# Attention with packed keys and a channel mix: first sequence by halves of its heads, weights' signs on ScalarE

## The chip, the cores and the metric

The kernel runs on one core of a Trainium2 chip. The time is device microseconds from launch to end; three runs of the kernel before gave 596.43, 597.06 and 598.03 (median 597.06). Beside these runs one execution was recorded by the profiler; its span, from the first to the last instruction, is 594.0 us. Engines: TensorE (PE, with its weight load PEld), VectorE (DVE), ScalarE (ACT), GpSimd (POOL), SyncE (SP, which issues DMAs).

## The reference

Shapes: batch 8, 8 heads, 576 rows, head size 64, 32 packed rows; model width 512, inner width 1024. All in fp32.

```python
def sm_attn(qq, kk, vv):
    s = scale * np.matmul(qq, kk.transpose(0, 1, 3, 2))
    s = s - np.max(s, axis=-1, keepdims=True)
    a = np.exp(s)
    a = a / (np.sum(a, axis=-1, keepdims=True) + 1e-09)
    return np.matmul(a, vv)
p_packed = sm_attn(p, k, v)
out = sm_attn(q, p_packed, p_packed)
# heads side by side: x is (8, 576, 512); x_prev is x one row later, zero first
xk = mu_k * x + (1.0 - mu_k) * x_prev
xr = mu_r * x + (1.0 - mu_r) * x_prev
k = np.maximum(xk @ w_k, 0.0)
v = k * k @ w_v
r = 1.0 / (1.0 + np.exp(-(xr @ w_r)))
return r * v
```

The three weights arrive as float64 (two 32-bit words each).

## The kernel before

The 8 x 576 rows are cut into nine blocks of 512 rows for the channel mix, so a block spans two sequences except for the first, which lies in the first sequence alone. Of a block TensorE makes `gates` (4 tiles of 128 rows against w_r, 4 parts of the width each), `keys` (8 tiles of the inner width) and `values` (8 x 4 tiles). Each of these 80 groups is three fp32r products of 128x512, because every operand is kept as a high and a low part (`_h`, `_l`): 240 products a block, in lines 936 to 938, 976 to 978 and 1005 to 1007.

A sequence's attention stands between them. k and q come in pairs of heads, are turned so that the head size lies on the partitions (for sequences 1 and 2 by TensorE, `transposed_on_pe` and `first_transposed`; for the others by VectorE in blocks of 32, `transposed`), `front` makes the first scores against p (line 503), `weights_of` the softmax, line 532 the packed rows, `scores` (for the first sequence `half_scores`, which takes half of the rows at a time) the second scores, `back` their softmax. Line 746 puts the result into x, and `mix` makes xk and xr from it. In the first sequence mu is multiplied into the packed rows (`shared`), and `mixed_on_pe` (line 806) lets TensorE make xk and xr directly from the attention weights `a2t`; `rest_of_first` makes the last 65 columns of x.

`convert` turns a piece of a weight (128 x 512 float64, loaded as `st`) into fp32: ScalarE scales the upper word (line 309), VectorE shifts it (311), puts the sign in (313), adds the top bits of the lower word (315); ScalarE writes the high part (319) and VectorE the low one (321). There are 20 pieces: 4 of w_r, 8 of w_k, 8 of w_v.

Nothing of the order is left to a scheduler on the chip: `Flow` runs the whole program as a list of parts, each with a rank, keeps an estimated clock for each engine, and writes the instruction that it thinks can start first. The numbers RANK_..., FIRST, HOLD_V and HOLD_S set ranks and patience. While TensorE has no work in the head, `fill` writes small products of the identity matrix (`spare`, line 1085), until the fourth tile of the first block's gates. Small pools of buffers (raw 3, kq 4, vt 2, staged 4, PSUM pa 2 and m 4) decide when loads and products may start. SP issues every DMA, by line 227.

## Time and profile before

| | us |
|---|---|
| median of three runs | 597.06 |
| span of the profiled execution | 594.0 |
| TensorE busy | 584.2 (98%) |
| VectorE busy | 370.9 (62%) |
| ScalarE busy | 309.2 (52%) |
| first gate product / last product of all | 37.67 / 589.93 |

A busy share is an average over stages with different limits, and products overlap in TensorE, so that one takes longer (about 0.39 us) than the distance to the next. For TensorE the distance from start to start is therefore what counts. An fp32 product (a fill, a score) stands in the trace as two passes: 78 fills in the program are 156 in the trace.

### The profile page before, as it was taken

The numbers are of one execution on the slowest core, as the hardware profiler recorded it, in microseconds if no ns is written. First come the engines' busy times: TensorE is split into PE (matmuls) and PEld (weight loads), VectorE is DVE, ScalarE is ACT, GpSimd is POOL, SyncE is SP. The second block draws the span as 40 slices with busy tenths as digits, with TensorE's granted clock in tenths as the row PEclk, the third lists the DMA queues.
The fourth block names the chain that finished last, engine by engine and source line by source line (L and its number), as shares of the span: only waits on it lengthen the run. The fifth ranks groups of instructions, "written<-read, shape, count | busy, mean of one in ns | idle before, by whom it ended". The sixth has DMA issues, their size and how long they took to land.

```text
span 594.0 us, 10276 instructions
## 1 busy us (share of the span) xinstructions
PE 584.2 (98%) x3965; PEld 458.9 (77%) x3965; DVE 370.9 (62%) x721; ACT 309.2 (52%) x548; POOL 2.1 (0%) x22
## 2 busy tenths in 40 slices
PE   9999999999999999999999999999999999999997
PEld 8776767787778777777777787777788888888885
DVE  2698999956692788867874698269314712641321
ACT  3557884644663458468537392548425613721410
POOL 0000000000000000000000000000000000000000
PEclk9999999999999999999999999999999999999999
DMA  8988460764727076486076375200100010001001
GB/s 214 266 207 258 164 139 17 162 173 73 150 46 189 12 154 143 129 143 141 3 195 135 65 140 134 58 1 1 72 1 1 1 72 0 1 0 72 0 1 71
DMA packets 164095, 56.51 MB, mean 95 GB/s; under 512 B 141000, under 2 KB 155344, under 8 KB 164048
## 3 DMA queue, kind: packets, MB, share of 16 engines
q1 hardware_dynamic: 164048, 55.87, 39.3%
q8 instruction: 31, 0.51, 0.4%
q14 instruction: 16, 0.13, 0.1%
HBM read 42.86 MB, written 12.98 MB: 94 GB/s over the span
## 4 chain that ended last, share of the span: by engine, by line
PE 80%; DVE 13%; SPq 3%; DMA 1%; issue 1%; ACT 1%; DVEq 0%
PE ph L936 10%; PE pvo L1005 10%; PE ph L937 10%; PE ph L938 10%; PE pvo L1007 10%; PE pvo L1006 10%; PE pr L976 5%; PE pr L977 5%; PE pr L978 5%; SPq L227 3%; DVE m L313 2%; DVE m L315 2%; PE pa L532 2%; PE pa L746 2%; PE pa L687 1%
## 5 line engine op out<-in xcount | busy, mean ns | idle before, releaser
L936 PE MATMUL ph<-xk,wk_h 128*128 128x512 f32 x288 | 114.8, 399 | 0.0
L1005 PE MATMUL pvo<-wv_h,sq 128*128 128x512 f32 x288 | 113.8, 395 | 0.0
L937 PE MATMUL ph<-xk,wk_h 128*128 128x512 f32 x288 | 112.5, 391 | 0.0
L938 PE MATMUL ph<-xk,wk_l 128*128 128x512 f32 x288 | 112.3, 390 | 0.0
L1006 PE MATMUL pvo<-wv_l,sq 128*128 128x512 f32 x288 | 112.2, 389 | 0.0
L1007 PE MATMUL pvo<-wv_h,sq 128*128 128x512 f32 x288 | 112.1, 389 | 0.0
L954 DVE CAST sq<-r 128x512 fp32r<-128x512 f32 x72 | 30.0, 416 | 122.0 <-ACT r L950 119.4
L947 ACT ACTIVATE r<-ph 128x512 f32<-128x512 f32 x72 | 43.0, 597 | 85.8 <-PE ph L938 85.5
L1005 PEld LDWEIGHTS pvo<-wv_h,sq 128*128 128x128 f32 x288 | 54.0, 188 | 16.5 <-issue 5.4
L936 PEld LDWEIGHTS ph<-xk,wk_h 128*128 128x128 f32 x288 | 54.1, 188 | 16.0 <-issue 4.1
L1007 PEld LDWEIGHTS pvo<-wv_h,sq 128*128 128x128 f32 x288 | 54.1, 188 | 11.4
L938 PEld LDWEIGHTS ph<-xk,wk_l 128*128 128x128 f32 x288 | 54.1, 188 | 11.4
L937 PEld LDWEIGHTS ph<-xk,wk_h 128*128 128x128 f32 x288 | 54.1, 188 | 11.0 <-DVE xk L843 0.6
L1006 PEld LDWEIGHTS pvo<-wv_l,sq 128*128 128x128 f32 x288 | 54.1, 188 | 10.7
L976 PE MATMUL pr<-wr_h,xr 128*128 128x512 f32 x144 | 57.5, 399 | 0.4 <-DVE sig L1016 0.3
L901 DVE SCALAR_TENSOR_TENSOR x<-xt,mus,x 128x64 f32<-128x64 f32 (+7 forms) x120 | 54.0, 495 | 6.0 <-ACT x L897 5.9
L977 PE MATMUL pr<-wr_l,xr 128*128 128x512 f32 x144 | 56.2, 390 | 0.0
L978 PE MATMUL pr<-wr_h,xr 128*128 128x512 f32 x144 | 56.1, 390 | 0.0
L897 ACT ACTIVATE x<-xt,mus 128x64 f32<-128x64 f32 (+7 forms) x120 | 54.4, 514 | 0.1
L987 ACT ACTIVATE sig<-pr 128x512 f32<-128x512 f32 x36 | 21.4, 601 | 60.7 <-PE pr L978 47.4
L956 DVE TENSOR_TENSOR sq<-r,sq 128x512 fp32r<-128x512 f32 x72 | 49.4, 686 | 1.4
L1016 DVE TENSOR_TENSOR sig<-pvo,sig 128x512 f32<-128x512 f32 x36 | 24.0, 687 | 39.0 <-PE pvo L1007 39.0
(102 smaller groups left out, 693.6 us busy)
## 6 DMA issues: line engine op xcount, KB each, us to landing
out<-sig SPq DMA_DIRECT2D x36, 256.0 KB, 2.6
raw<-in_k SPq DMA_DIRECT2D x96, 72.0 KB, 2.7
raw<-in_q SPq DMA_DIRECT2D x96, 72.0 KB, 2.8
st<-in_moe_w_k SPq DMA_DIRECT2D x8, 512.0 KB, 5.2
st<-in_moe_w_v SPq DMA_DIRECT2D x8, 512.0 KB, 4.7
vt<-in_v SPq DMA_DIRECT2D x24, 160.0 KB, 3.4
away<-blocks SPq DMA_DIRECT2D x12, 288.0 KB, 2.7
vt<-in_v SPq DMA_DIRECT2D x24, 128.0 KB, 3.8
```

The lines of the kernel that those rows point to most:

```text
L897: nc.scalar.mul(x32[:, o:o + n], xts[b, c][:, 1 + s:1 + s + n], mus[:, j, c:c + 1])
L901: nc.vector.scalar_tensor_tensor(x32[:, o:o + n], xts[b, c][:, s:s + n], mus[:, j + 1, c:c + 1], x32[:, o:o + n], op0=ALU.mult, op1=ALU.add,)
L936: nc.tensor.matmul(ph, wk_h[:, c, fs], xh, start=(c == 0), stop=False)
L937: nc.tensor.matmul(ph, wk_h[:, c, fs], xl, start=False, stop=False)
L938: nc.tensor.matmul(ph, wk_l[:, c, fs], xh, start=False, stop=(c == NC - 1))
L956: nc.vector.tensor_tensor(hl[:, 1, :], r, hl[:, 0, :].bitcast(F32), op=ALU.subtract)
L976: nc.tensor.matmul(pr, xh[:, ts_], wr_h[:, c, :], start=(c == 0), stop=False)
L977: nc.tensor.matmul(pr, xh[:, ts_], wr_l[:, c, :], start=False, stop=False)
L978: nc.tensor.matmul(pr, xl[:, ts_], wr_h[:, c, :], start=False, stop=(c == NC - 1))
L1005: nc.tensor.matmul(pv[t], sh, wv_h[:, f, :], start=(f == 0), stop=False)
L1006: nc.tensor.matmul(pv[t], sh, wv_l[:, f, :], start=False, stop=False)
L1007: nc.tensor.matmul(pv[t], sl, wv_h[:, f, :], start=False, stop=(f == NF - 1))
```

## The change

- The first sequence is worked by halves of its heads (`first_side(h)`, two pairs of heads each) and not by halves of its rows. Its loads come in the order k, q of pairs 0 and 1, k of pairs 2 and 3, v, q, v. p is loaded with zeros between its heads, so that two heads' 32 packed rows are one product of 64 columns; the packed rows are masked to a block diagonal.
- Its second scores lie token-major: 112 or 128 rows of q on the partitions and 64 columns for a pair's two heads (`CHUNKS`, 5 x 128 = 640 columns in all). The softmax runs along the free dimension without VectorE's transposes; TensorE turns the result back.
- mu is loaded broadcast over partitions by POOL's queue (`first_constants`), multiplied with the packed rows by VectorE, and `mixed_on_pe` makes two of the four parts of xr or xk with four products of 64 rows and 512 columns. The loads of p (first sequence) and of mu's rows are issued by ScalarE.
- `first_gates` does the first two parts of the width for three tiles, then the other two, then the fourth tile.
- In `convert` ScalarE scales the lower word in place (line 329 after), which leaves the top bits as an integer, and uses Prelu with a slope so that the sign comes with the scaling (331); VectorE joins both in one step (334). The limit 29.829 lets all 20 pieces go this way.
- EARLY = 1: k and q of the second sequence are loaded with 32 columns a time and turned by VectorE, as those of the later sequences; its attention works in blocks from there on.
- All ranks have new numbers, and some are added.

```diff
+    RANK_LATE7 = 3.494
...
+    def load(dst, src, issue, us, queue="queue"):
+        yield queue, issue, None, None
+        dict(queue=nc.sync, scalar=nc.scalar, gpsimd=nc.gpsimd)[queue].dma_start(dst, src)
...
-    EARLY = 2
+    EARLY = 1
...
+        pieces_split.append(event)
+        by_act = len(pieces_split) < RANK_LATE13
+        if by_act:
+            yield act(n)
+            nc.scalar.activation(w0, w0, AF.Copy, scale=2.0 ** -29 * (1 - 2.0 ** -22), bias=-0.5)
         yield act(n)
-        nc.scalar.activation(m.bitcast(F32), w1.bitcast(F32), AF.Copy, scale=2.0 ** -112)
-        yield vec2(n)
-        nc.vector.tensor_scalar(m, m, 3, None, op0=ALU.logical_shift_left)
-        yield vec(n, after=0.0)
-        nc.vector.scalar_tensor_tensor(m, w1, 0x80000000, m, op0=ALU.bitwise_and, op1=ALU.bitwise_or)
-        yield vec(n, after=0.0)
-        nc.vector.scalar_tensor_tensor(m, w0, 29, m, op0=ALU.logical_shift_right, op1=ALU.bitwise_or)
+        nc.scalar.activation(m.bitcast(F32), w1.bitcast(F32), AF.Prelu, scale=2.0 ** -112, alpha=2.0 ** 32)
+        if by_act:
+            yield vec(n)
+            nc.vector.scalar_tensor_tensor(m, m, 3, w0, op0=ALU.logical_shift_left, op1=ALU.bitwise_or)
+        else:
+            yield vec2(n)
+            nc.vector.tensor_scalar(m, m, 3, None, op0=ALU.logical_shift_left)
+            yield vec(n, after=0.0)
+            nc.vector.scalar_tensor_tensor(m, w0, 29, m, op0=ALU.logical_shift_right, op1=ALU.bitwise_or)
...
+    def first_loads():
+        flow.spawn(first_packed(), 5)
+        for h in range(2):
+            for j in (2 * h, 2 * h + 1):
+                flow.spawn(first_pair(k, "kT", j, "xk"), FIRST_K[h])
+                flow.spawn(first_pair(q, "qT", j, "xk" if j == NPR - 1 else "raw"), FIRST_Q[h])
+            flow.spawn(values_of(0, h), FIRST_V[h])
...
+    def first_side(h):
...
+        for hf in range(2):
+            for j, half in enumerate(HALVES):
+                nc.tensor.matmul(
+                    s1[half, hf, :HS], pts[0][1][:, j0 + j, :], ts["kT", 0, j0 + j][1][:, hf * HS:(hf + 1) * HS],
+                    start=True, stop=True,
+                )
...
+        yield from weights_of(0, h, slot, s1, sm)
...
+                nc.tensor.matmul(
+                    pv[rows], aT[:n, c, rows], vt[:n, pr, c * D:(c + 1) * D], start=(c == 0), stop=(c == 4),
+                )
...
+        nc.vector.scalar_tensor_tensor(
+            pm, pv.unsqueeze(1).broadcast_to([P, 2, D]), rs[:, h:h + 1], firsts["mask"], op0=ALU.mult, op1=ALU.mult,
+        )
...
+        nc.tensor.transpose(pT, pm, ident)
+        ppT = firsts["ppT"][:, h]
+        yield act(P)
+        nc.scalar.copy(ppT, pT)
...
+        s2 = banks(slot).rearrange("p a b -> p (a b)")
+        for k, (at, _) in enumerate(CHUNKS):
+            for j in range(2):
+                nc.tensor.matmul(
+                    s2[:, k * P + 64 * j:k * P + 64 * j + 64], ts["qT", 0, j0 + j][1][:, at:at + P],
+                    ppT[:, 64 * j:64 * j + 64], start=True, stop=True,
+                )
...
+        nc.vector.tensor_reduce(m2, s2, axis=AX.X, op=ALU.max)
+        yield vec(n)
+        nc.vector.tensor_tensor(e, s2, over, op=ALU.subtract)
+        flow.give("pa", slot)
+        yield act(n, table="exp")
+        nc.scalar.activation(e, e, AF.Exp, scale=scale)
+        yield vec(n)
+        nc.vector.tensor_reduce(m2, e, axis=AX.X, op=ALU.add)
...
+        nc.vector.tensor_tensor(e, e, over, op=ALU.mult)
...
+        for k, (at, rows) in enumerate(CHUNKS):
+            bank, col = (0, at) if k < 4 else (1, 0)
+            nc.tensor.transpose(back_[:, bank, col:col + rows], e[:rows, k], ident[:rows, :rows])
+        flow.give("xk", se)
+        a2 = firsts["a2"][1][:, h]
+        last = CHUNKS[4][0]
+        yield act(last)
+        nc.scalar.copy(a2[:, 1:1 + last], back_[:, 0, :last])
+        yield act(S - last, after=0.0)
+        nc.scalar.copy(a2[:, 1 + last:], back_[:, 1, :S - last])
...
+        for j, res, tag in ((2, xrs, "xr"), (0, xks, "xk")):
+            flow.spawn(mixed_on_pe(h, j, res, tag), RANK_MIX if tag == "xr" else RANK_KEYS)
...
+        for h in range(2):
+            firsts["mu", h] = (yield from flow.take("sig"))
+        for h in range(2):
+            t = tile_([P, 4, P], F32, "sig", firsts["mu", h], "mub")
+            for j, mu in ((2, mu_r), (0, mu_k)):
+                for c in range(2):
+                    at = (2 * h + c) * P
+                    yield from load(
+                        t[64 * c:64 * c + 64, j], mu[at:at + P].unsqueeze(0).broadcast_to([64, P]), 1.0, 0.02, "gpsimd"
+                    )
...
+        nc.vector.tensor_scalar(t[:, 1::2], t[:, 0::2], -1.0, 1.0, op0=ALU.mult, op1=ALU.add)
...
+        nc.vector.tensor_tensor(t, t, pm.unsqueeze(1).broadcast_to([P, 4, P]), op=ALU.mult)
...
-    def mixed_on_pe(hf, j, res, tag, first):
...
+    def mixed_on_pe(h, j, res, tag):
...
+        slot = yield from flow.take("pa")
+        yield pe(2.0)
+        px = banks(slot)
+        for t in range(2):
+            for c, half in enumerate(HALVES):
+                nc.tensor.matmul(
+                    px[:, c, :TB], shares_of[half, j + t, :], a2[half, h, 1 - t:1 - t + TB], start=(t == 0), stop=(t == 1),
+                )
...
+            yield act(TB, after=multiplied)
+            nc.scalar.copy(xh, x)
+            yield vec(TB)
+            nc.vector.tensor_tensor(xl, x, xh.bitcast(F32), op=ALU.subtract)
...
+        opened = []
+        for part, (cs, tiles) in enumerate(((range(2), range(3)), (range(2, 4), range(3)), (range(4), range(3, 4)))):
+            for t in tiles:
+                if part != 1:
+                    slot = yield from flow.take("m")
+                    opened.append((slot, ps.tile([P, DM], F32, name="pr", tag=f"m{slot}")))
+                slot, pr = opened[t]
+                ts_ = slice(t * P, (t + 1) * P)
+                for c in cs:
+                    yield from flow.wait(("xr", 0, c), ("wr", c, 0))
+                    if part == 1 and flow.keep_busy:
+                        flow.keep_busy = 0.0
+                        flow.give("m", 3)
+                    yield pe(0.683)
+                    flow.now.t -= flow.LAG
+                    _, xh, xl = xrs[0, c]
+                    nc.tensor.matmul(pr, xh[:, ts_], wr_h[:, c, :], start=(c == 0), stop=False)
+                    nc.tensor.matmul(pr, xh[:, ts_], wr_l[:, c, :], start=False, stop=False)
+                    nc.tensor.matmul(pr, xl[:, ts_], wr_h[:, c, :], start=False, stop=(c == NC - 1))
```

On TensorE, from the first scores of the second kind (`qT`, `ppT`) to the first gate products, before:

```order
L667 MATMUL pa<-qT,ppT 32x288 x8
L455 MATMUL pq<-ident,raw 128x96 x6
L1085 MATMUL spare<-ident 128x128 x5
L667 MATMUL pa<-qT,ppT 32x288 x8
L1085 MATMUL spare<-ident 128x128 x20
L415 MATMUL pa<-ident,raw 128x96 x6
L1085 MATMUL spare<-ident 128x128 x2
L415 MATMUL pa<-ident,raw 128x96 x6
L1085 MATMUL spare<-ident 128x128 x5
L806 MATMUL pa<-a2t,pms 64x288 x16
L1085 MATMUL spare<-ident 128x128 x7
L976 MATMUL pr<-wr_h,xr 128x512
```

Now, at the same place (`both` holds the packed rows, `e` the attention weights, `mub` mu times the packed rows; line 610 the scores, 643 the turning back, 956 the mixing products, 1112 the gates), from the second half's scores on:

```order
L610 MATMUL pa<-both,qT 128x64 x10
L643 MATMUL pa<-ident,e 128x112 x4
L643 MATMUL pa<-ident,e 128x128
L1248 MATMUL spare<-ident 128x128 x4
L956 MATMUL pa<-a2t,mub 128x512 x4
L1248 MATMUL spare<-ident 128x128 x9
L1112 MATMUL pr<-wr_h,xr 128x512
```

The second sequence's transposes (`ident,raw`) are gone from this place, and the first half's turning back stands behind the second half's scores.

On ScalarE, from the exp of the first sequence's second softmax (`e`) to the first gate input (`xr`), before (418 copies turned k, 309 and 319 are conversions):

```order
L713 ACTIVATE e<-e 128x576
L418 COPY kT<-pa 128x576
L319 CAST wr_h<-m 128x512
L418 COPY kT<-pa 128x576
L841 CAST xr<-pa 128x288 x4
```

Now:

```order
L628 ACTIVATE e<-e 128x640
L329 ACTIVATE st<-st 128x512
L331 ACTIVATE m<-st 128x512
L329 ACTIVATE st<-st 128x512
L600 COPY both<-pT 128x128
L331 ACTIVATE m<-st 128x512
L329 ACTIVATE st<-st 128x512
L343 CAST wr_h<-m 128x512
L331 ACTIVATE m<-st 128x512
L343 CAST wr_h<-m 128x512
L648 COPY a2t<-pa 128x448
L650 COPY a2t<-pa 128x128
```

Eight conversion steps of w_r now stand between the exp and the copies of the first half's attention weights; three more and the second half's exp follow before the first `xr`.

On VectorE, around the last product of that softmax, before (722 the last product, 725 the transpose behind it) and then now (636 the last product; 334 and 345 are conversions):

```order
L720 RECIPROCAL m_441<-m_441 128x18
L711 TENSOR_TENSOR e<-e,m_473 128x576
L722 TENSOR_TENSOR e<-e,m_441 128x576
L315 SCALAR_TENSOR_TENSOR m<-st,m 128x512
L725 STREAM_TRANSPOSE a2t<-e 128x2x288
```

```order
L634 RECIPROCAL m_364<-m_364 128x20
L334 SCALAR_TENSOR_TENSOR m<-m,st 128x512
L636 TENSOR_TENSOR e<-e,m_364 128x640
L695 TENSOR_TENSOR mub<-mub,pm 128x512
L334 SCALAR_TENSOR_TENSOR m<-m,st 128x512
L345 TENSOR_TENSOR wr_l<-m,wr_h 128x512
```

A conversion step stands ahead of the product, and no transpose behind it.

## Rows read from the trace of the kernel before

**Rows 1.** The page's first part: busy us, share of the span, instructions.

```profile
PE 584.2 (98%) x3965; PEld 458.9 (77%) x3965; DVE 370.9 (62%) x721; ACT 309.2 (52%) x548; POOL 2.1 (0%) x22
```

**Rows 2.** Timeline of TensorE, end: start, us, line, out<-in, shapes, count [idle before].

```profile
587.66 0.39 PE L1006 MATMUL pvo<-wv_l,sq 128*128 128x512 f32 x1
...
589.93 0.39 PE L1007 MATMUL pvo<-wv_h,sq 128*128 128x512 f32 x1
```

**Rows 3.** Timeline of TensorE, the head.

```profile
11.46 1.20 PE L503 MATMUL pa<-kT,pt 64*32 64x288 f32 x32
...
17.89 0.90 PE L532 MATMUL pa<-vt,aT 128*32 128x64 f32 x40
...
20.43 0.33 PE L553 MATMUL pa<-ident,pm 128*128 128x128 f32 x1
...
23.88 0.71 PE L667 MATMUL pa<-qT,ppT 64*32 64x288 f32 x16
...
27.40 4.73 PE L1085 MATMUL spare<-ident 128*128 128x128 f32 x40
...
34.67 1.48 PE L806 MATMUL pa<-a2t,pms 32*64 32x288 f32 x32
...
37.67 0.47 PE L976 MATMUL pr<-wr_h,xr 128*128 128x512 f32 x1
```

**Rows 4.** Windows: stretch, us, busy PE, PEld, DVE, ACT, POOL, PEclk, DMA share, GB/s.

```profile
7.00:20.00 13.00, 12.28 (x199) 10.60 (x198) 3.74 (x10) 6.06 (x13) 0.00 (x0) 1.00 0.84 206
...
20.00:116.00 96.00, 92.43 (x796) 68.46 (x793) 91.41 (x184) 65.96 (x130) 0.30 (x3) 1.00 0.64 173
```

**Rows 5.** Timelines of VectorE and TensorE where the second block's gates start.

```profile
114.69 0.69 DVE L919 TENSOR_TENSOR xr<-x,xr 128x512 fp32r<-128x512 f32 x1
...
116.31 0.47 PE L976 MATMUL pr<-wr_h,xr 128*128 128x512 f32 x1
```

**Rows 6.** SP's timeline, then loads of q and k to 26 us: ns min/median/max, landing.

```profile
1.18 4.94 SPq L227 DMA_DIRECT2D raw<-in_k  x8
...
L227 SPq DMA_DIRECT2D raw<-in_q x8: 430/569/1852, 10.7 to 17.6; - x8
...
DMA to landing us min/median/max: 2.8/3.6/6.7
```

**Rows 7.** Lines by form of VectorE: busy us, mean ns of one | idle before.

```profile
L400 DVE STREAM_TRANSPOSE kT<-raw 128x576 f32<-128x576 f32 x24 | 17.7, 752 | 0.0
L315 DVE SCALAR_TENSOR_TENSOR m<-st,m 128x512 uint32<-128x512 uint32 x20 | 13.8, 688 | 0.4
...
L722 DVE TENSOR_TENSOR e<-e,m 128x576 f32<-128x576 f32 x16 | 11.8, 744 | 0.0
...
L311 DVE TENSOR_SCALAR m<-m 128x512 uint32<-128x512 uint32 x20 | 8.3, 415 | 5.3 <-ACT m L309 5.3
```

**Rows 8.** Lines by form of ScalarE.

```profile
L768 ACT COPY xt<-pa 128x576 f32<-128x576 f32 x28 | 30.9, 1167 | 23.5 <-PE pa L746 23.3
...
L309 ACT ACTIVATE m<-st 128x512 f32<-128x512 f32 x20 | 13.4, 686 | 6.1 <-DMA st<-in_moe_w_r 2.7 <-DMA st<-in_moe_w_v 1.8 <-DMA st<-in_moe_w_k 1.4
...
L713 ACT ACTIVATE e<-e 128x576 f32<-128x576 f32 x16 | 10.8, 680 | 7.2 <-DVE e L711 7.2
```

**Rows 9.** Timeline of TensorE after the gates' start: where other work stands between products.

```profile
40.59 0.48 PE L976 MATMUL pr<-wr_h,xr 128*128 128x512 f32 x1
...
42.14 1.37 PE L806 MATMUL pa<-a2t,pms 32*64 32x224 f32 x32
...
46.59 0.72 PE L806 MATMUL pa<-a2t,pms 32*64 32x288 f32 x8
...
48.82 0.50 PE L976 MATMUL pr<-wr_h,xr 128*128 128x512 f32 x1
...
72.38 1.45 PE L415 MATMUL pa<-ident,raw 96*128 96x96 f32 x12
...
85.67 1.21 PE L687 MATMUL pa<-qT,ppT 64*32 64x288 f32 x32 [0.16 <-ACT ppT L556]
```

More of the change, by code (lines that the diff above doesn't have):

```diff
@@ L416, in transposed_on_pe @@
         flow.give(raw_space, raw_slot)
-        yield act(S)
-        nc.scalar.copy(t.rearrange("p (a b) -> p a b", a=2), pT[:, :, :HS])
+        if b == 0 and pr < RANK_LATE14:
+            done = flow.t
+            yield vec(HS)
+            nc.vector.tensor_copy(t[:, :HS], pT[:, 0, :HS])
+            one = flow.t
+            yield act(HS, after=done)
+            nc.scalar.copy(t[:, HS:], pT[:, 1, :HS])
+            flow.now.t = max(flow.t, one)
+        else:
+            yield act(S)
+            nc.scalar.copy(t.rearrange("p (a b) -> p a b", a=2), pT[:, :, :HS])
         flow.give("pa", slot)
@@ L484, in packed, with first_packed @@
         flow.set(("pt", b))
+    def first_packed():
+        sp = yield from flow.take("tmp")
+        pin = tile_([P, NPR, 2, NP], F32, "tmp", sp, "pin")
+        nc.gpsimd.memset(pin, 0.0)
+        for o in range(0, P, 32):
+            hh, dh = divmod(o // 32, 2)
+            yield from load(
+                pin[o:o + 32, :, hh, :],
+                p[0, hh::2, :, 32 * dh:32 * dh + 32].rearrange("pr n d -> n pr d"),
+                0.5, 0.1, "scalar",
+            )
+            if o < 96:
+                back_to_issue("scalar")
+        slot = yield from flow.take("tmp")
+        pt = tile_([P, NPR, 2 * NP], F32, "tmp", slot, "pt")
+        yield vec(2 * P)
+        nc.vector.transpose(pt.rearrange("p a b -> p (a b)"), pin.rearrange("p a r b -> p (a r b)"))
+        flow.give("tmp", sp)
+        pts[0] = slot, pt
+        flow.set(("pt", 0))
@@ L801, in first_products @@
-    def first_products(px, n, a2, terms):
-        for term, (at, weights) in enumerate(terms):
-            for pr in range(NPR):
-                own = slice(32 * pr, 32 * pr + 32)
-                for h, half in enumerate(HALVES):
-                    nc.tensor.matmul(
-                        px[pr // 2][half, pr % 2, :n], weights(own, h), a2[own, h, at:at + n],
-                        start=(term == 0), stop=(term == len(terms) - 1),
-                    )
-    def mixed_on_pe(hf, j, res, tag, first):
-        a2 = first["a2"][1]
-        yield from flow.wait("pms")
+    def mixed_on_pe(h, j, res, tag):
+        a2 = firsts["a2"][1]
+        yield from flow.wait(("pms", h))
@@ L815, in mixed_on_pe @@
         if tag == "xk":
             yield from flow.wait(("mixed", 1, "xr"))
[L818 to L819 removed]
+        shares_of = firsts["shares", h]
         space = "xk" if tag == "xk" else "sq"
[L821 to L826 removed]
@@ new lines, in mixed_on_pe @@
+        flow.set(("mixed", h, tag))
+        multiplied = flow.t
+        for c in range(2):
+            sx = yield from flow.take(space)
+            hl = tile_([P, 2, TB], F32R, space, sx, tag)
+            xh, xl = hl[:, 0, :], hl[:, 1, :]
+            x = px[:, c, :TB]
+            yield act(TB, after=multiplied)
+            nc.scalar.copy(xh, x)
+            yield vec(TB)
+            nc.vector.tensor_tensor(xl, x, xh.bitcast(F32), op=ALU.subtract)
+            if c:
+                flow.give("pa", slot)
+            res[0, 2 * h + c] = sx, xh, xl
+            flow.set((tag, 0, 2 * h + c))
@@ new lines, in rest_of_first @@
+    def rest_of_first():
+        n = S - TB
+        yield from flow.wait(*(("mixed", h, tag) for h in range(2) for tag in ("xr", "xk")))
+        sx, a2 = firsts["a2"]
+        slot = yield from flow.take("pa")
+        yield pe(0.7)
+        px = banks(slot)
+        for h in range(2):
+            for c, half in enumerate(HALVES):
+                nc.tensor.matmul(
+                    px[:, c, h * P:h * P + n + 1], firsts["pm", h][1][half], a2[half, h, TB:], start=True, stop=True,
+                )
+        for h in range(2):
+            flow.give("pm", firsts["pm", h][0])
+            flow.give("sig", firsts["mu", h])
+        flow.give("sig", firsts["both"])
@@ L1039, in all_loads @@
     def all_loads():
-        for b in range(B):
+        first_loads()
+        for b in range(1, B):
             flow.now.rank = lrank(b)
@@ L1078, in attn_pack_channel_mix @@
     weights()
[L1079 removed]
+    flow.spawn(first_constants(), 10.01)
+    flow.spawn(shares(), RANK_LATE12)
     flow.spawn(channel_mix(), 50)
```

305 lines of the change are left out of this document (153 added, 152 removed).

## The prediction

> **What bounds the kernel now.** I read the page first: TensorE is busy for 98% of the span [rows 1]. Busy is no verdict, so next came the pitch of the product stream. In its steady part ten 128x512 products start in 2.27 us (587.66 to 589.93), 0.227 us each [rows 2]. The channel mix needs 9 blocks x 240 = 2160 of them, 490.3 us. The first gate product starts at 37.67 [rows 3], the last product of all at 589.93 [rows 2]: 552.3 us, so about 62 us of TensorE after 37.67 go to other things (attention of the later sequences, the first sequence's mix, waits). The tail behind 589.93 is 4.1 us. So the span is start of the gates + 490.3 + the other work + tail, and the change can move only the first and the third.
>
> The head is a chain of latencies: fills keep TensorE busy while it waits (40 passes of them at 27.40) [rows 3]. The windows show which engine it waits for: from 20 to 116 us VectorE is busy 91.4 of 96 us, ScalarE 66.0 [rows 4]. At the end of that stretch is a second meeting point: the last part of the second block's gate input leaves VectorE at 114.69 + 0.69, and the second block's gates start at 116.31 [rows 5], so this part is ready some 3 us before the fourth product group needs it. A gain in the head would be lost there again if VectorE kept its work.
>
> **The change, part by part.**
>
> *The head (term A).* Before, the first score products wait for eight k loads, issued over 4.94 us [rows 6], and start at 11.46; the products with v start at 17.89, the second scores at 23.88, the mixing products at 34.67, the gates at 37.67 [rows 3]. Afterwards one half of the heads goes ahead alone. Four k loads fewer bring its start 2.5 us forward, to 9.0. From 11.46 to 17.89 stand 6.4 us for both halves; one half saves one max (0.74) [rows 7]: 5.7. The products with v take 0.9 [rows 3], the scaling behind them 0.4 (17.89 + two such sets and what lies between, to 20.43), the other half's products, which now stand ahead on TensorE, 1.2 (the price of 32 passes of 288 columns) [rows 9], the transpose 0.33 and its copy 0.3 [rows 3]: 17.8. Transposes of the other heads' q in front cost 0.5: 18.3. The token-major scores (10 products, 20 passes, each with its own 128 columns of weights and 64 moving columns) are in no row. A fill pass of 128 moving columns takes 0.118 us [rows 3], so 20 passes take 2.4 at most, and half of that, by columns, at least; the weights are the fill's, so I take the middle, 1.8: 20.1. The softmax over 640 columns goes by the rows of 576: max 0.83, subtraction 0.83, exp 0.76, sum 0.83, small steps 0.4, a conversion step ahead of the last product 0.69, product 0.83: 5.2, 25.3 [rows 7, 8]. Five transposes, 0.7: 26.0. Two copies on ScalarE stand behind up to three conversion steps (1.7) and take 0.8: 28.5. The four mixing products of 64 rows and 512 columns: 8 passes of 4 x 0.118 [rows 3], two side by side, 1.9: 30.4. Cast 0.6, subtraction 0.69: 31.7. Hand-offs not in the blocks above, some twelve at 0.05, 0.6: the gates start at 32.3. A = 37.67 - 32.3 = 5.4. The weights don't set this: k, q and v of the first sequence are 3.5 MB and the first piece of w_r 0.5; at 206 GB/s [rows 4] they are in by about 21, and the other three pieces come at 2.5 us each.
>
> *TensorE after the start of the gates (term B).* What goes: the transposes of the second sequence, 2.24 between the first two groups of three gate products (37.67 to 40.59, less 0.68), 1.3 at 72.38, and two lots of six later at half of that; 4.8. The rest of the first sequence's mix: 1.37 at 42.14, 2.23 from 46.59 to 48.82 with its wait for VectorE, and a like set later which I price the same; 5.8 [rows 3, 9]. What comes: five transposes 0.7, three sets of mixing products 5.7 and, from the order of instructions, two waits, 0.5 before the second gate input and 0.6 before the last mixing set; 7.5. B = 10.6 - 7.5 = 3.1. The attention of sequences two to eight costs TensorE the same as before.
>
> *Conversions.* A piece loses two VectorE steps, 0.42 and 0.69 [rows 7], and gains a ScalarE step. VectorE: -22.1 for 20 pieces, +6.0 for eight transposes of the second sequence [rows 7], +1.5 for four copies of k at half a row of 576: 91.4 becomes about 77, in a stretch that is to shrink from 96 to 87 us. So the meeting point at 116 can move with TensorE, and no part of A and B is handed back there. ScalarE: the added step works in place on every second word, which no row shows. Below it lies the neighbouring scaling step, 0.69; above it the copies in blocks, 1.17 for 576 columns [rows 8]. I take 0.69, the like operation: +13.7, less 5.4 for eight copies and about 1 elsewhere: 66.0 becomes some 74 of 87. That cover is gone at 13 us more. Prelu in place of Copy has the same two ends, and I price it as Copy.
>
> *Second sequence in blocks.* Its 32 loads read 128-byte runs in place of 16 with 256-byte ones. The DMA engines are at 64% from 20 to 116 us [rows 4], so I cost the bytes at nothing; 16 more issues at the old spacing of 0.62 us [rows 6] are 10 us of SP, which would show as w_k arriving late, against a bound of nothing below.
>
> *Loads on other queues.* p and the rows of mu are issued by ScalarE, mu's copies by POOL; no row has either. On SP a load takes 0.43 to 1.85 us to issue and 2.8 to 6.7 to land [rows 6]. Four p loads from about 2.2 are out at 4.0 at the lower end and in by 7.6, before 9.0. POOL's first four are in between 6 and 16; VectorE has them ahead of its first max (10), so the upper end costs 6 us, the lower none, and I take none.
>
> Sum: 5.4 + 3.1 = 8.5 us. Against the profiled execution's own span, 594.0, that is 585.5; the median of the runs, 597.06, lies 3.0 above that span (what lies around it), hence 588.5.
>
> **The rivals.**
>
> (1) *ScalarE fills the head.* If the in-place step costs 1.17, four of them stand ahead of the first gate input (1.9) and nine more before the gates end, on an engine that has no idle time there: about 5 us back, 593.5. For it: ScalarE has the conversions and the copies of the first sequence in one queue. Against: the like step takes 0.69.
>
> (2) *ScalarE becomes the bound, and the kernel slower.* If both scalings of a piece are dear, 40 steps decide, up to the second block's gates. 74 of 87 us leave 13, 0.33 a step; the gain is another 0.21. Above 0.69 + 0.54 = 1.23 us a step the kernel is slower; at 1.3 it is 3 us, 600. Against: that is above the dearest such row (1.17). For: nothing but that neither step has been run.
>
> (3) *POOL's loads are late.* VectorE's sixth instruction waits for the first four; landing at 16 shifts the whole head by 6: 594.5. For: no DMA of POOL is in the trace. The Trainium skill has a rule that would do this ("SBUF — State Buffer", "SBUF: two separate sides"): while VectorE runs an operation in a two-port mode, POOL cannot write the descriptors of its own DMAs. No run here shows it; by the order of instructions VectorE has only copies out of PSUM and one transpose at that time, so the chance stays small.
>
> (4) *The 64-row products don't run two at a time.* Each mixing set then costs 3.8 and not 1.9: 7.6 more, 596. Against: 32 passes of 288 columns on 64x32 tiles take 1.21 [rows 9], 0.038 each where one alone needs more than a fill's 0.118; so tiles of 64 rows do run side by side.
>
> (5) *No change.* The second meeting point does not move (a late chain of the second sequence, whose loads and transposes now compete for SP and VectorE): 596 to 598.
>
> **How the numbers follow.** Forecast 0.70, own range 583 to 592.5 (scores 0.6 either way, hand-offs and waits 2, a partly slower ScalarE step 2). Rival 1 0.12, rival 2 0.06, rival 3 0.04, rival 4 0.04, rival 5 0.04. A measurement of this kernel tells 0.3%, 1.8 us, from no change. Faster by more than that (below 595.3): 0.70 + 0.12 + 0.04 and half of rival 4, 0.88; same 0.06; slower 0.06. The range that should hold eight in ten reaches up over rivals 1 and 3 and down to the forecast's own end: 583 to 594.5.
>
> **What would show it.** In the profile afterwards the first gate product starts near 32; between it and the first key product lie no waits above about 1 us; VectorE's busy time from 20 us to the second block's gates falls to about 77; the added ScalarE step has a mean below 0.75; VectorE's wait for POOL's loads is under 1 us; the second block's gates start near 107. The prediction is wrong if the gates start after 35, if either scaling takes over 1 us, or if key products wait for w_k, xk or a free bank.

## The result, and the profile after

The changed kernel takes 586.52 us, median of 4 runs (585.96 to 587.72), against 597.37 us of the kernel before beside it (596.43 to 598.03). The ratio is 0.9824, with a 95% interval from 0.9809 to 0.9839: faster by 1.8%. Forecast were 588.5 us and a range from 583 to 594.5. The profiled span goes from 594.0 to 584.0 us.

The page's first part of the changed kernel, busy us and share of the span, answers to [rows 1]:

```profile
PE 576.0 (99%) x3746; PEld 452.8 (78%) x3746; DVE 358.9 (61%) x687; ACT 315.9 (54%) x554; POOL 7.3 (1%) x36
```

VectorE loses 12 us over the whole span, ScalarE gains 7, TensorE has 219 instructions fewer. None of these numbers is the gain; the times on TensorE are. Its timeline in the head, for [rows 3]:

```profile
8.60 1.19 PE L555 MATMUL pa<-kT,pt 128*64 128x288 f32 x8
...
14.23 0.90 PE L576 MATMUL pv<-vt,aT 128*32 128x64 f32 x40 [0.38 <-DMA vt<-in_v]
15.06 1.19 PE L555 MATMUL pa<-kT,pt 128*64 128x288 f32 x8
16.18 0.33 PE L597 MATMUL pT<-ident,pm 128*128 128x128 f32 x1
...
17.30 2.37 PE L610 MATMUL pa<-both,qT 128*128 128x64 f32 x20
...
24.51 2.44 PE L610 MATMUL pa<-both,qT 128*128 128x64 f32 x20
26.80 0.67 PE L643 MATMUL pa<-ident,e 112*128 112x112 f32 x5
...
28.28 1.99 PE L956 MATMUL pa<-a2t,mub 64*128 64x512 f32 x8
30.20 2.27 PE L1248 MATMUL spare<-ident 128*128 128x128 f32 x18
32.23 0.47 PE L1112 MATMUL pr<-wr_h,xr 128*128 128x512 f32 x1
```

The second scores of the first half start at 17.30, those of the other half at 24.51; the first gate product stands at 32.23, where [rows 3] have 37.67. Behind it, TensorE's other work between the gate products (for [rows 9]) and the start of the second block's gates (for [rows 5]):

```profile
37.50 3.71 PE L956 MATMUL pa<-a2t,mub 64*128 64x512 f32 x16
...
42.60 1.99 PE L956 MATMUL pa<-a2t,mub 64*128 64x512 f32 x8 [0.49 <-DVE xr L969]
...
45.41 0.66 PE L985 MATMUL pa<-a2t,pm 64*128 64x65 f32 x8
...
105.79 0.39 PE L1134 MATMUL pr<-wr_h,xr 128*128 128x512 f32 x1
...
579.89 0.39 PE L1165 MATMUL pvo<-wv_h,sq 128*128 128x512 f32 x1
```

From first gates to second gates are 73.56 us, before 78.64. The 10.0 us of the span are 5.44 in front of the first gate product, 5.08 between there and the second block's gates, and 0.5 given back behind them. The tail behind the last product is 4.1 us as before.

The windows (stretch, us, busy PE, PEld, DVE, ACT, POOL, PEclk, DMA share, GB/s) answer to [rows 4]:

```profile
20.00:37.70 17.70, 17.70 (x161) 14.86 (x160) 17.47 (x34) 15.54 (x31) 0.00 (x0) 1.00 1.00 258
20.00:107.00 87.00, 85.96 (x638) 63.98 (x636) 78.27 (x147) 75.63 (x140) 0.31 (x3) 1.00 0.80 194
```

Up to the second block's gates VectorE is busy 78.27 us of 87, ScalarE 75.63: forecast were 77 and 74. The two scalings of a piece, by form on ScalarE over that stretch, stand at the price of [rows 8]'s scaling:

```profile
L329 ACT ACTIVATE st<-st 128x512 uint32<-128x512 uint32 x20 | 13.2, 679 | 0.0
L331 ACT ACTIVATE m<-st 128x512 f32<-128x512 f32 x20 | 13.2, 672 | 0.0
```

TensorE's waits between 32 and 110 us (total, times, longest) are down to three:

```profile
PE pa L956 <- DVE xr L969: 0.5, 1, 0.5
PE pa L802 <- ACT a L788: 0.3, 1, 0.3
PE pvo L1163 <- ACT r L1079: 0.2, 1, 0.2
```

### The profile page after: what moved, and what is told of

It reads as the page before. It is cut to its first block, busy times and chain, and to the rows that moved or that the text cites. A ratio compares the mean times of both kernels' runs of the same rounds, so it can differ in the third digit from the quotient of the medians.

```text
span 584.0 us, 9831 instructions
## 1 busy us (share of the span) xinstructions
PE 576.0 (99%) x3746; PEld 452.8 (78%) x3746; DVE 358.9 (61%) x687; ACT 315.9 (54%) x554; POOL 7.3 (1%) x36
## 4 chain that ended last, share of the span: by engine, by line
PE 81%; DVE 8%; ACT 5%; DMA 2%; issue 2%; SPq 1%; DVEq 0%; ACTq 0%
PE ph L1068 10%; PE pvo L1163 10%; PE ph L1069 10%; PE ph L1070 10%; PE pvo L1164 10%; PE pvo L1165 10%; PE pr L1134 5%; PE pr L1135 5%; PE pr L1136 5%; DVE x L1033 2%; PE pa L911 2%; PE pa L739 1%; SPq L242 1%; PE pa L715 1%; PE pa L864 1%
## 5 line engine op out<-in xcount | busy, mean ns | idle before, releaser
L1163 PE MATMUL pvo<-wv_h,sq 128*128 128x512 f32 x288 | 114.0, 396 | 0.2 <-ACT r L1079 0.2
L1163 PEld LDWEIGHTS pvo<-wv_h,sq 128*128 128x128 f32 x288 | 54.1, 188 | 17.8 <-issue 6.3
L1070 PEld LDWEIGHTS ph<-xk,wk_l 128*128 128x128 f32 x288 | 54.1, 188 | 11.4
L1165 PEld LDWEIGHTS pvo<-wv_h,sq 128*128 128x128 f32 x288 | 54.1, 188 | 11.4
L1134 PE MATMUL pr<-wr_h,xr 128*128 128x512 f32 x128 | 50.5, 395 | 0.0
L1135 PE MATMUL pr<-wr_l,xr 128*128 128x512 f32 x128 | 49.9, 390 | 0.0
L1136 PE MATMUL pr<-wr_h,xr 128*128 128x512 f32 x128 | 49.8, 389 | 0.0
L1082 ACT ACTIVATE r<-r 128x512 f32<-128x512 f32 x72 | 45.4, 631 | 2.1
```

The costliest lines, as they stand in the source:

```text
L1070: nc.tensor.matmul(ph, wk_l[:, c, fs], xh, start=False, stop=(c == NC - 1))
L1134: nc.tensor.matmul(pr, xh[:, ts_], wr_h[:, c, :], start=(c == 0), stop=False)
L1135: nc.tensor.matmul(pr, xh[:, ts_], wr_l[:, c, :], start=False, stop=False)
L1136: nc.tensor.matmul(pr, xl[:, ts_], wr_h[:, c, :], start=False, stop=(c == NC - 1))
L1163: nc.tensor.matmul(pv[t], sh, wv_h[:, f, :], start=(f == 0), stop=False)
L1165: nc.tensor.matmul(pv[t], sl, wv_h[:, f, :], start=False, stop=(f == NF - 1))
```

## The experiments

The numbers that set the order (the ranks) were found for one set of parts. In unpaired and double_step every instruction keeps its place. In six kernels (k_first, turn_pe, conv_undone, before_conv, before_turn, old_head) the planner makes its order anew from the same numbers, apart from the edit shown. In four more, pool_sub and those whose names end in _r, the numbers were chosen anew, by a search for the earliest end of the planner's own plan. The table has the ratio to the kernel before with its 95% interval, the profiled span, and the starts of the gates of blocks one to four on TensorE's timeline.

| kernel | ratio | span | block 1 | block 2 | block 3 | block 4 |
|---|---|---|---|---|---|---|
| before | 1 | 594.0 | 37.7 | 116.3 | 177.8 | 240.9 |
| changed | 0.9824 [0.9809, 0.9839] | 584.0 | 32.2 | 105.8 | 166.8 | 231.9 |
| unpaired | 0.9827 [0.9798, 0.9856] | 583.5 | 31.6 | 105.2 | 166.1 | 231.3 |
| double_step | 0.9971 [0.9955, 0.9987] | 592.3 | 33.3 | 114.0 | 174.9 | 240.1 |
| k_first | 0.9972 [0.9945, 0.9998] | 593.0 | 37.3 | 105.8 | 168.2 | 240.8 |
| turn_pe | 0.9997 [0.9979, 1.0015] | 595.2 | 31.9 | 111.1 | 172.1 | 242.8 |
| turn_pe_r | 0.9933 [0.9909, 0.9956] | 590.6 | 34.0 | 113.0 | 175.8 | 239.2 |
| conv_undone | 1.0583 [1.0552, 1.0614] | 628.7 | 32.0 | 155.0 | 217.7 | 280.1 |
| conv_undone_r | 1.0134 [1.0112, 1.0155] | 601.3 | 33.5 | 122.8 | 183.9 | 248.4 |
| before_conv | 0.9999 [0.9979, 1.0019] | 593.7 | 38.1 | 116.1 | 177.1 | 242.4 |
| before_turn | 1.0334 [1.0306, 1.0362] | 614.4 | 36.3 | 135.2 | 201.1 | 263.4 |
| old_head | 1.0124 [1.0092, 1.0156] | 601.9 | 37.4 | 113.9 | 176.7 | 250.6 |
| old_head_r | 0.9992 [0.9972, 1.0012] | 595.1 | 36.4 | 116.2 | 177.2 | 244.0 |
| pool_sub | 0.9939 [0.9918, 0.9960] | 590.6 | 32.9 | 113.4 | 176.3 | 238.8 |

**Do two products of 64 rows run side by side?** The mixing set's price and rival 4 rest on it. Every instruction keeps its place; only the order inside the set changes.

```
-        for t in range(2):
-            for c, half in enumerate(HALVES):
+        for c, half in enumerate(HALVES):
+            for t in range(2):
```

> The changed kernel with the four products of a mixing set in another order, both of one half of the rows and then both of the other, so that neighbours on TensorE no longer use different rows; order and everything else as it was. Theory (two products of 64 rows run side by side, 1.99 us a set): only the middle pair still overlaps, (8 - 1) x 0.47 = 3.3 us a set, up to 3.8 if none does; four sets make 5.2 to 7.2 us: first gate product at 33.5 to 34, 592.3 us, 591 to 594. Rival (they never ran side by side; the 1.99 us come from cheaper passes): no change, 586 to 587.5 us.

Measured: 585.61 us, no change. The first set and then the two sets that stand together, on TensorE's timeline of this kernel:

```profile
27.66 2.00 PE L956 MATMUL pa<-a2t,mub 64*128 64x512 f32 x8
...
36.88 3.81 PE L956 MATMUL pa<-a2t,mub 64*128 64x512 f32 x16
```

The first set takes 2.00 us where the changed kernel's takes 1.99: the rival was right, alternating the rows buys nothing. Eight more passes cost 3.71 - 1.99 = 1.72 us in the changed kernel, 0.215 us a pass of 512 columns. The stream's products of 512 columns start 0.227 us apart, one behind the other [rows 2], so this price leaves nothing for an overlap to explain. The prediction had built its 0.47 us from four fill passes of 128 columns (0.118 each [rows 3]); but a pass of the scores with 64 columns takes as much (2.37 us for 20), so that price comes with the pass and not with its columns.

One way out remains: that TensorE rearranges what it is given and runs pairs in both orders. The Trainium skill ("TensorE: Matmul & The Clock Gate", "The mechanism") has weights for rows not in use pulled ahead, but products starting and ending strictly in program order. By that rule most of an overlap would have been lost in the new order, and the time did not change. The traces show the equal times and the price of a pass; a kernel with products on one half alone was not run.

**How much room has ScalarE?** A step whose result is not needed is added to each converted piece; the order stays.

```
             nc.scalar.activation(w0, w0, AF.Copy, scale=..., bias=-0.5)
+            nc.scalar.activation(m.bitcast(F32), w1.bitcast(F32), AF.Prelu, ...)
```

> The changed kernel with a second, idle ScalarE step (0.67 us) in each piece converted with ScalarE's help, on the same words as the step ahead of it. 20 of them fall between 20 us and the second block's gates: 75.6 + 13.6 = 89 of 87 us. Theory (ScalarE has 11 us of cover and no more, and less in the head): the gates start 1 to 2 us late, the second block's gates 3 to 6 us late: 591 us, 588.5 to 594. Rival 1 (ScalarE has more room than its busy time shows): 586 to 588 us. Rival 2 (ScalarE is already the bound and every step counts): 598 to 601 us.

Measured: 594.38 us, 0.4 above the theory's range. TensorE's waits between 30 and 115 us of this kernel (two largest):

```profile
PE pa L803 <- ACT a L789: 2.0, 1, 2.0
PE pa L957 <- DVE xr L970: 0.8, 1, 0.8
```

The first gates are 1.07 us late, as the theory has it, the second block's 8.2, where it has 3 to 6. So 20 steps of 0.67 us, 13.4 us in all, cost 8.2, though the window counts 11.4 us of idle time on ScalarE. The idle time is not where the steps stand: from 20 to 37.7 us it has 2.2 us, and the first extra waits come on exponentials and copies that queue behind the conversions.

**Is the start of the gates the thing to shorten?** All k loads go first, so v and q of the first half land later.

```
-    RANK_LATE2 = 7.09
+    RANK_LATE2 = -1.0
```

> The changed kernel with all eight k loads of the first sequence ahead of q and v, so that q and v of the first half of the heads are issued four loads later. Theory (the head is a chain whose next links after the first scores are the landings of v and q): at 0.62 us an issue v and q land 2.5 us later; the products with v start at 16 to 17 and not at 14.23, the first gate product at 34 to 35: 588.7 us, 588 to 590. Rival (the loads have slack, softmax and conversions set the head): first gates within 0.7 us of 32.23, 586 to 587.3 us.

Measured: 593.78 us; theory and rival both missed, at the first gates (37.26) and in the time. TensorE's timeline of this kernel:

```profile
15.55 0.90 PE L576 MATMUL pv<-vt,aT 128*32 128x64 f32 x40 [1.62 <-DMA vt<-in_v]
...
30.71 1.99 PE L956 MATMUL pa<-a2t,mub 64*128 64x512 f32 x8
32.62 0.71 PE L643 MATMUL pa<-ident,e 112*128 112x112 f32 x5
...
35.35 1.99 PE L956 MATMUL pa<-a2t,mub 64*128 64x512 f32 x8 [0.45 <-ACT a2t L650]
37.26 0.50 PE L1112 MATMUL pr<-wr_h,xr 128*128 128x512 f32 x1
...
105.82 0.47 PE L1134 MATMUL pr<-wr_h,xr 128*128 128x512 f32 x1
```

The products with v wait for their load and start 1.3 us late (15.55 against 14.23), not 2.5. The first mixing set is 2.43 us late (30.71 against 28.28), so about half of its delay arises behind the landings, and the gates start 5.03 us later. Yet the second block's gates start at the same time: the planner has put one mixing set and five transposes ahead of the gates, where TensorE ran fills, and a set of first scores that cost 1.3 us behind the second block's gates (it stands at 102.48 in the changed kernel). Counted at block 3 the late head cost 1.4 us (168.2 against 166.8). So the start of the gates alone is no measure; what TensorE has left to do behind it belongs to it.

Another 7.5 us are lost between block 3 and block 4. The windows of this kernel there:

```profile
166.00:170.00 4.00, 2.82 (x13) 2.00 (x11) 3.81 (x8) 3.04 (x7) 0.00 (x0) 1.00 0.62 100
170.00:173.00 3.00, 1.20 (x4) 0.67 (x4) 3.00 (x8) 2.73 (x6) 0.10 (x1) 0.85 1.03 360
173.00:178.00 5.00, 4.14 (x75) 2.65 (x75) 5.00 (x13) 3.60 (x8) 0.10 (x1) 0.50 0.68 152
178.00:182.00 4.00, 4.00 (x35) 2.38 (x35) 1.00 (x4) 1.52 (x2) 0.00 (x0) 0.50 0.48 75
```

TensorE's waits there, on its timeline:

```profile
170.29 0.50 PE L1136 MATMUL pr<-wr_h,xr 128*128 128x512 f32 x1 [1.48 <-DVE xr L1051]
...
173.13 0.80 PE L1134 MATMUL pr<-wr_h,xr 128*128 128x512 f32 x1 [1.64 <-ACT xr L1049]
...
175.08 0.79 PE L1136 MATMUL pr<-wr_h,xr 128*128 128x512 f32 x1 [0.73 <-DVE xr L1051]
```

TensorE waits 3.8 us for the third block's xr (VectorE begins the first of its low halves at 169.55, the gates are due at 168.20; in the changed kernel it begins at 161.57). In the second of these waits, at about 172 us, the granted clock falls to 0.50, the 1.2 GHz level, and stays there for about ten microseconds; two neighbouring products then start 0.43 us apart (179.16 and 179.59) in place of 0.227. Waits and half clock are what these rows have to set against the 7.5 us. The same place costs 5.6 us in turn_pe and 8.7 in old_head (block 3 to 4: 70.7 and 73.9 us against 65.2). Both have waits and then a clock of 0.50 there: in old_head 3.8 us for the same xr, in turn_pe 3.2 us of the next sequence's attention (2.2 for pm, 1.0 for a load). That is why the numbers were chosen anew in the runs below whose names end in _r.

**What is turning on VectorE worth?** The second sequence goes back to TensorE, first with the old numbers, then with new ones.

```
-    EARLY = 1
+    EARLY = 2
```

> The changed kernel with k and q of the second sequence turned by TensorE again, from 256-byte loads. Theory (TensorE is the bound from the gates on): its list grows by 5.0 us, what the transposes and their waits took in the kernel before: 591.5 us, 590 to 593; the first gate product stays near 32.2. Rival (they would stand in TensorE's waits, and VectorE 6.0 us lighter pays for them): 586 to 588 us.

Measured: 595.87 us, above the theory's range. The gates start at 31.95, the second block's 5.3 us later than in the changed kernel, as the theory has it; and 5.6 of the other 5.9 us fall between block 3 and 4, the place just named.

```
+    EARLY = 2
-    RANK_LATE13 = 29.829
+    RANK_LATE13 = 20
...
```

> The changed kernel with k and q of the second sequence turned by TensorE, as before (595.9 us), with the numbers that set the order chosen anew, the number of pieces that ScalarE helps to convert among them (19 in place of 28). Theory: the 5.3 us that it is late at the second block's gates stay, since TensorE's list has them; the 5.6 us lost between the third and fourth block's gates go: 590.5 us, 589 to 592. Rival 1 (with an order that fits, TensorE's transposes cost nothing): 586 to 588 us. Rival 2 (the order is not the cause): 595 us.

Measured: 592.18 us, 0.2 above the theory's range. ScalarE helps with 19 of the 20 pieces here (L329 x19 in this trace). The loss between block 3 and 4 is gone (63.4 us); the theory's 5.3 are 7.2 at block 2 in this order, of which 1.7 stand in front of the first gates (33.95), and 7.3 at block 4. Neither rival holds: with an order of their own, the transposes on TensorE still cost 1.1% (0.9933 / 0.9824).

**What is the new conversion worth?** The old one is put back into the changed kernel.

```
-        if by_act:
-            nc.scalar.activation(w0, w0, AF.Copy, ...)
-        nc.scalar.activation(m.bitcast(F32), w1.bitcast(F32), AF.Prelu, ...)
-        ...
+        nc.scalar.activation(m.bitcast(F32), w1.bitcast(F32), AF.Copy, scale=2.0 ** -112)
+        nc.vector.tensor_scalar(m, m, 3, None, op0=ALU.logical_shift_left)
+        nc.vector.scalar_tensor_tensor(m, w1, 0x80000000, m, op0=ALU.bitwise_and, ...)
+        nc.vector.scalar_tensor_tensor(m, w0, 29, m, op0=ALU.logical_shift_right, ...)
```

> The changed kernel with the old conversion (three VectorE steps, one ScalarE step a piece). Theory: VectorE has to do about 100 us of work where 87 us stand (78.3 + 20 x 1.1), all of it ahead of the second block's gates; these start 8 to 15 us later, the first gates within 1.5 us of 32.23: 598 us, 593 to 604. Rival (VectorE's load matters little, head and TensorE's list give the gain): 586 to 589 us.

Measured: 630.90 us, much worse than the theory. TensorE's waits between 30 and 156 us:

```profile
PE pa L795 <- ACT a L781: 12.8, 2, 10.5
PE pa L904 <- DVE a L896: 9.4, 1, 9.4
```

From 70 to 110 us the granted clock is 0.60. With the numbers chosen anew:

> The changed kernel with the old conversion (three VectorE steps a piece), as before (630.9 us), with the numbers that set the order chosen anew. Theory (VectorE has to do 100 us of work in 87 of which it has 9 idle): the second block's gates are some 13 us late, at 115 to 121 and not at 155, and no long wait is left that lets the clock fall: 599 us, 595 to 604. Rival 1 (with an order that fits, the old conversion is as good): 586 to 589 us. Rival 2 (the price does not depend on the order): 620 us or more.

Measured: 604.10 us, 0.1 above the theory's range. The window to the second block's gates of this kernel:

```profile
20.00:122.80 102.80, 95.36 (x692) 71.35 (x692) 98.26 (x186) 67.64 (x122) 0.31 (x3) 0.98 0.64 159
```

VectorE is busy 98.3 of 102.8 us, and TensorE runs fills between the first block's gates (5.07 us of them from 50.77) and waits 2.7 us, in three places, for low halves of w_r from VectorE. So VectorE's work holds the second block's gates, 17 us later than in the changed kernel. Inside the change this part is worth 3.2% (1.0134 / 0.9824) at these two orders, and most of what the 630.9 lost, 27 of 44 us, was order and clock.

**What are the parts worth alone?** Three kernels start from the kernel before: the conversion alone, the turning alone, both together (then with the numbers chosen anew). The new head alone was not run.

```
before_conv:   the convert() of the changed kernel
before_turn:   -    EARLY = 2        +    EARLY = 1
old_head:      both
```

> The kernel before with the new conversion alone (ScalarE makes the low words and the signs for 28 of the 36 pieces, VectorE one step of three). Theory (head and TensorE's own list give the time; the conversion only makes room): VectorE loses some 22 us between 20 us and the second block's gates (91.4 to about 69), yet the first gate product stays within 1 us of 37.67 and TensorE gets back only its waits for VectorE, 0.4 + 0.7 + 0.4 us: 595.5 us, 594 to 597. Rival (VectorE's load was the bound all along and the conversion is the gain): 586 to 590 us.

Measured: 595.54 us, as the theory has it. VectorE falls from 91.4 to 75.8 us between 20 and 116 us (the theory has 69), and the kernel gains nothing. The pieces are 20, and all 20 go the new way (L314 and L316 x20 in this trace), not 28 of 36 as the expectation says.

> The kernel before with k and q of the second sequence turned by VectorE in blocks, the old conversion kept. Theory (VectorE full at 91.4 of 96 us): 5.0 us of transposes leave TensorE, but VectorE gets 6.0 us more and the second block's gates wait for it; of the 5.0 at most 1 arrives: 597 us, 595.5 to 600. Rival (TensorE's list alone counts): 592 us.

Measured: 616.39 us; the direction is the theory's, the size is not. The window of this kernel to the second block's gates:

```profile
20.00:135.20 115.20, 96.60 (x757) 70.43 (x756) 105.04 (x206) 67.13 (x127) 0.31 (x3) 0.91 0.65 158
```

VectorE is busy 105.0 of 115.2 us, converted pieces come late (TensorE waits 8.0 us for wv_h and wv_l alone), and the mean clock of the stretch is 0.91. This kernel was not given an order of its own, so how much of the loss is order stays open.

> The kernel before with the new conversion and with k and q of the second sequence turned by VectorE, everything of the change but the new head (and its loads on other queues). Theory: TensorE loses 5.0 us of transposes and some 1 us of waits, VectorE has room for it (91.4 - 22 + 6 = 75 of 90): 591.3 us, 590 to 593, first gate product near 37.5; the rest to the changed kernel, about 5 us, is the head. Rival 1 (the head's gain is swallowed later, the rest is the gain): 586 to 588 us. Rival 2 (the head is all of it): 595 to 597 us.

Measured: 603.17 us, outside the theory and both rivals. The second block's gates come at 113.9, 2.4 us earlier than before. Between block 3 and 4 8.7 us are lost against the changed kernel and 10.9 against the kernel before; the next expectation gives 10.8 as the loss against the changed kernel, which is not so.

> The kernel before with the new conversion and with k and q of the second sequence turned by VectorE, as before (603.2 us), but with the numbers that set the order chosen anew for it. Theory (that kernel lost 10.8 us between the third and the fourth block's gates, 176.7 to 250.6 against 166.8 to 231.9 in the changed kernel, to waits for xr and the half clock behind them, because its order was set for other parts): no waits above 1 us there, second block's gates at 112 to 114, first gates near 37: 592 us, 590 to 594.5; what is left to the changed kernel's 586.5, about 5.5 us, is the head. Rival 1 (the head gives nothing): 586 to 588 us. Rival 2 (the order is not the cause): 600 us or more.

Measured: 595.64 us, outside the theory and both rivals. The loss at block 3 is mostly gone (66.8 us to block 4, 63.0 in the kernel before), but the second block's gates are back at 116.2. ScalarE's two largest waits between 30 and 117 us in this kernel, and TensorE's two:

```profile
ACT st L314 <- DMA st<-in_moe_w_v: 5.0, 1, 5.0
ACT st L314 <- DMA st<-in_moe_w_k: 3.9, 3, 1.9
```

```profile
PE pa L815 <- ACT a L601: 2.4, 2, 1.6
PE ph L945 <- ACT xk L850: 1.7, 1, 1.7
```

TensorE has 5 us of transposes less and waits 5.4 us for ScalarE in this stretch (these two and 1.3 us for r), which itself waits 8.9 us for weights to land. That the one comes from the other fits the times (ScalarE's longest wait ends at 63.47, a wait of TensorE for it ends at 72.11) but was not tested. With the old head, in the two orders tried, conversion and turning together give nothing.

**Can GpSimd take work from the two full engines?** ScalarE and VectorE are near full up to 107 us, GpSimd is idle.

```
-        nc.vector.tensor_tensor(lo[:, c, o:o + n], m..., hi[...], op=ALU.subtract)
+        nc.gpsimd.tensor_tensor(lo[:, c, o:o + n], m..., hi[...], op=ALU.subtract)
```

> The changed kernel with the last step of each conversion, the subtraction that makes the low half, done by GpSimd (7.3 us busy in the whole span) and the numbers that set the order chosen anew. It takes 0.69 us a piece from VectorE, which is busy 17.47 of 17.7 us ahead of the second mixing set and 78.3 of 87 up to the second block's gates; in that time TensorE waits 1.5 us and the rest of its list stays. Theory (VectorE holds the head's end and these waits): 584.5 us, 582.5 to 587. Rival (GpSimd takes above 2 us a piece, or slows VectorE's operations beside it, so that converted pieces come late): 588 to 600 us.

Measured: 592.46 us: the rival's time, and by the second of its two reasons; GpSimd stays under 2 us a piece, but VectorE's operations beside it are slowed. GpSimd's timeline in the head, then VectorE's, in this kernel, and last VectorE's in the changed kernel:

```profile
23.22 1.27 POOL L347 TENSOR_TENSOR wr_l<-m,wr_h 128x512 fp32r<-128x512 f32 x1 [16.65 <-ACT wr_h L344]
25.92 1.50 POOL L347 TENSOR_TENSOR wr_l<-m,wr_h 128x512 fp32r<-128x512 f32 x1 [1.42 <-ACT wr_h L344]
```

```profile
23.86 0.67 DVE L636 TENSOR_SCALAR m<-m 128x20 f32<-128x20 f32 x1
...
26.20 1.78 DVE L699 TENSOR_TENSOR mub<-mub,pm 128x512 f32<-128x512 f32 x1
```

```profile
23.05 0.18 DVE L632 TENSOR_SCALAR m<-m 128x20 f32<-128x20 f32 x1
...
24.98 0.69 DVE L695 TENSOR_TENSOR mub<-mub,pm 128x512 f32<-128x512 f32 x1
```

In the changed kernel the same two take 0.18 and 0.69 us. Here the first ends at 24.53, as GpSimd's operation ends at 24.49, and the second 0.56 us after GpSimd's end at 27.42: both times VectorE's operation is done only once GpSimd's is. The Trainium skill ("SBUF — State Buffer", "SBUF: two separate sides") has the rule: the two share a port pair, and whichever of certain operations starts first holds it for the whole instruction. The trace agrees for these two; a copy out of PSUM beside the first (23.50) takes 0.43 us, no more than elsewhere. VectorE is still busy 16.91 of 17.7 us in the head with four operations fewer. From 20 to 107 us its busy time falls from 78.27 to 71.81 us, less than half of the 13.8 that 20 steps of 0.69 would free. Part of the 7.6 us at block 2 may be the new order; that was not separated.

## Why the prediction was right, and where it was not

**Term A, the head: right in sum, not in its parts.** Forecast was a first gate product at 32.3 and A = 5.4; measured 32.23 and 5.44. That these agree so closely is luck: errors of a microsecond and more, told below, cancel, and in unpaired, with every instruction in the same place, the same product starts at 31.61. The half starts at 8.60 and not 9.0, pT is turned from 16.18, where the forecast has 17.2 (its 17.8 less the transpose and the copy), and the wait for q (0.26 us) holds the scores at 17.30. These take 2.37 us, the upper bound 2.4, where 1.8 was taken. The softmax takes 5.35 of the forecast 5.2 (19.71 to 24.25 + 0.81). The five transposes then start at 26.80, not 25.3: they stand behind the other half's scores (24.51 + 2.44), which the sum did not price. The late transposes were made good by the copies: these were priced at 2.5 us, 1.7 of it for three conversion steps in front of them, but ScalarE had done these steps before the late transposes ended, and the copies start 0.03 us after the transposes' end (L648 on ScalarE at 27.50). The mixing products start at 28.28, 0.2 ahead of the forecast, and take 1.99 of forecast 1.9.

**The price of the mixing set was right for a wrong reason.** "8 passes of 4 x 0.118 [rows 3], two side by side" gives 1.9; measured are 1.99, in eight passes of 0.215 to 0.25 that do not depend on the exchange of neighbours. Two errors of a factor of two met. The right price stood in [rows 2]: eight times the 0.227 us between 512-column products is 1.8, with no overlap at all. Rival 4 was no danger: without the overlap that it takes away, the set costs the same. The argument against it, from 32 passes on tiles of 64x32, does not carry over to tiles of 64x128.

**Term B: 3.1 forecast, 5.08 measured less 0.5 later.** The gaps between the 512-column products, less one pitch of 0.227 each, sum to 24.2 us before and 19.1 after. Of the 24.2, each with the restart behind it, the second sequence's transposes are 4.9 (forecast 4.8) and the first sequence's mix 7.0 (forecast 5.8: the last strip of 0.5 and some 0.1 us of restart behind each insert were left out). What comes is 8.3 (forecast 7.5; fills between the gates, 0.46, and the same restarts). That makes 3.6 of the 5.08. The rest, some 1.5, are waits and restarts in the attention of the second and third sequence that are gone, such as the 0.16 us for ppT in [rows 9]; the prediction priced that attention as unchanged. In all the span lost 10.0 us where the sum has 8.5, and the term most off is B.

**Conversions: prices right, the room wrong.** 0.679 and 0.672 us a step against 0.69 forecast, and VectorE at 78.27 against 77. The step that failed is "that cover is gone at 13 us more": 13.4 us more cost 8.2 at the second block's gates. The threshold of rival 2 was put too high with it. In double_step 13.4 us cost 8.3 of span; if every further one costs its full length, the 10 us of gain are used up after some 15 us, 0.38 us for each of 40 steps, at about 1.06 us a step and not 1.23. This is an estimate from that one run.

**The meeting point moved, as forecast, and this part is where the change is decided.** The second block's gates start at 105.79, forecast near 107. conv_undone_r shows the other case: the meeting point stays with VectorE, 17 us later. The prediction's words, that no part of A and B is handed back, are shown for this order alone; k_first, with the same parts in another order, lost 7.5 us behind block 3. Leaving one part out of the change costs 3.2% (conversion), 1.1% (turning) and 1.7% (head, old_head_r), 6% in all, for a gain of 1.8%; adding one to the kernel before gives nothing (conversion) or makes it 3.3% slower (turning, in the old order). The terms do not add up part by part: the conversion alone frees VectorE for nothing, and the turning needs that room.

**Loads and POOL: nothing was late.** VectorE's operation on POOL's loads starts at 8.34 without a wait, no key product waits for w_k, and the DMA share rises from 0.64 to 0.80 at no visible cost in this kernel. The other queues were not tested by themselves; what p and mu on SP would cost stays open.

**Open:** the orders chosen anew may not be the best for their parts, so the prices of the parts above are upper bounds of what each is worth. How much of the loss of pool_sub and of before_turn is order is open too, and so is what the new head is worth without the other two parts.

## What to carry to other kernels

An engine's idle time in a window is not room: it counts only where the queue in front of the next needed result has it, so test the room with added steps before building on it. Parts that each relieve another engine are to be priced together and in the order they will run in; an order found for one set of parts cost another set 4 to 27 us here. And a price that fits the sum is not yet a mechanism: two loops exchanged took the supposed mechanism away and left the price.

## What the hardware showed unexpectedly

- A pass of TensorE in fp32 with 128 columns of weights takes 0.118 us whether 64 columns move (scores, 2.37 us for 20) or 128 (fills [rows 3]); one of 64 rows and 512 columns takes 0.215 to 0.25, whether its neighbour uses the same rows or not.
- In k_first TensorE's granted clock fell from 1.00 to 0.50 during the second of two waits (1.48 and 1.64 us, four products between them) and stayed there for some ten microseconds, a third wait of 0.73 us among them: 3.8 us of waits, with this stretch behind them, stand against 7.5 us lost.
- A GpSimd subtraction of 128x512 takes 1.27 to 1.75 us in the head of pool_sub, and two VectorE operations beside it went from 0.18 to 0.67 and from 0.69 to 1.78 us.
